# A Fourier and state-space mix on one core: the first loads from another queue, the vectors prepared later, a retuned order

## The chip, the cores and the metric

The kernel runs on one core of a Trainium2 chip. The metric is device time in microseconds (us) of one execution; the kernel before takes 328.49 us in the median of three runs (327.45, 328.49 and 333.03). The core's engines work at the same time, each through its own queue in order: TensorE (PE; its weight loads are listed as PEld), VectorE (DVE), ScalarE (ACT), GpSimd (POOL) and SyncE (SP). DMAs are issued from the queues of SP, ACT and POOL.

## The reference: what is computed

The input x has 2048 rows (tokens) and 1024 columns. Two results are computed from it and mixed by a gate, one number per token:

```python
g = sigmoid((x * gate_w).sum(-1, keepdims=True))
a = irfft2(rfft2(x) * (w_r + 1j * w_i))            # over both axes
Lam_bar = exp(exp(log_dt) * Lam)                   # 1024 complex states
h[t] = Lam_bar * h[t-1] + x[t] @ B_bar.T           # over 2048 steps
b = 2 * real(h @ C.T) + x * Dskip
out = g * a + (1 - g) * b
```

So `a` filters x in the frequency domain, and `b` is a diagonal state-space model with complex states. The five vectors that the change speaks of are Lambda_re, Lambda_im, log_dt, Dskip and gate_w, of 1024 elements each.

## The kernel before, in words

Both transforms are written as matrix products with constant cosine and sine matrices. x comes in as eight pairs of row blocks (`load_x`, line 206), sixteen blocks of 128 x 1024 in all. In the text the blocks are T0 to T15, and the steps of the first stage are called by the letters that the kernel uses:

- **T** (`turn_x`, lines 725 to 730): PE transposes a block in eight products into a PSUM tile `pt` (four buffers), ACT copies it into `xQ`. What the state-space part later multiplies is `xQ`, and it needs all sixteen blocks.
- **f** (`fold`, lines 732 to 745): DVE adds and subtracts halves of the block (`preT`, `sums`).
- **F** (`fd`, lines 353 to 367): eight products of the folded block with the constant `G` (the transform over columns) into a PSUM tile, which DVE or ACT copies into `X1` (line 364; DVE for blocks 0, 3, 5, 10 and 15).
- **S** (`s1`, lines 369 to 387): four products with the constant `T2`, a copy by DVE or ACT into `A1` (line 385), and a DMA to a scratch in DRAM.
- **h** (`unit`, lines 311 to 327): 32 products of `xQ` with B, a copy by ACT. After two of them DVE has a list of pieces for the recurrence (`recur`, lines 263 to 309: multiplications, scans), taken off the list by **v** (`vector`, line 332) as far as the next number of `SHARE` allows.
- **a** (`small`, line 901) and **t** (`make_tab`, line 219): small arithmetic on the five vectors, and the tables of the recurrence, on ACT, DVE and POOL.
- **g** (`gate`, line 778): 32 products for the gate, a copy by ACT.
- **b**, **c**, **2**, **w**, **k** issue loads; **s** is a step of the rest of the Fourier part; **|** marks the end of the table work.

F, S, g and the throwaway products write to one pool of two PSUM buffers (`psA`, tag "ps"), so a product has to wait until the copy of the tile before the last is done.

The order in which PE, DVE and ACT get their instructions is written out by hand in the string `ORDER` (lines 39 to 45), one letter per step; each engine executes its share of it strictly in turn. SP and POOL are ordered by a planner. After the string, the early tiles, the late tiles and the output follow in loops.

Ahead of the string stands the start (lines 756 to 772): eight throwaway products on zeros (`keep_warm(8)`), the loads, T0, f0, T1, f1, four more throwaway products, F0. Then come lines 848 to 867: the five vectors, which line 185 loads from ACT's queue as the first DMAs of all, are transposed by PE into a tile `vps` of the `pt` pool and turned into `vecT`, `vecF`, `gw32`, `dt`, `are`, `thp` and `r_sb` by DVE and ACT.

Of the kernel before, what the change touches and what calls it, by code (L numbers as in the profile page):

```python
# [32 lines left out]
    3.3, 6.2, 1.8, 5.9, 1.6, 0.9, 2.9, 1, 3.4, 4, 2.5, 5.4, 0, 4.8, 2.2, 4.1,  # L33
    2.1, 1.5, 6.8, 1.3, 3.8, 3.8, 2.7, 1.2, 6.2, 2.3, 4, 4.7, 1.8, 0.7, 2.8, 0.8,
    4.1, 4.9, 2.9, 6.4, 1.5, 3.8, 4, 1.6, 1.4, 2.5, 3.3, 1.8, 4.2, 2.7, 0.4, 0,
    4.4, 1.7, 4.8, 0, 2.4, 5.5, 3.5, 5.1, 4.2, 4.3, 4.7, 3.2, 4.3, 1.6, 6.7, 5,
    1.1, 4.1, 2.1, 7.1, 4.8, 4.3, 5.9,
)
ORDER = (
    "FTfSTbTTFTSbfbfbTTFfTSfTbbFbTbfbTwSTSTFTf2baFfabaSxatfbbbFhtStbt",  # L40
    "tfFfbStthttFShStttthfFfkttFtvttthtStvgSfFcFttShtvtcvtthtttcSFtth",
    "ttvFtcStttStt|cvvsccdchvhvvehvshhvshvhvshvhvshvsshvshvsshvshvssh",
    "vsvhshsvshvsshshvsvshvshvsshvsvhsshvshvshvhvhvsvshvsvshvsvshsvvs",
    "hvsvvshsvshvsivshvsvsvh",
# [74 lines left out]
def kernel(  # L119
# [64 lines left out]
    for i, src in enumerate((B_Lambda_re, B_Lambda_im, B_log_dt, B_Dskip, gate_w)):  # L184
        nc.scalar.dma_start(out=vec8[:, i, :], in_=src.rearrange("(j p) -> j p", p=P))
# [162 lines left out]
    def gfnet():  # L348
# [4 lines left out]
        def fd(j):  # L353
# [10 lines left out]
            (nc.vector.tensor_copy if j in (0, 3, 5, 10, 15) else nc.scalar.copy)(  # L364
# [391 lines left out]
    keep_warm(8)  # L756
    load_x(0, slice(0, 1))
    load_x(0, slice(1, 2))
    for part in (slice(0, 4 * K), slice(4 * K, 4 * K + 4 * H)):
        nc.sync.dma_start(out=fft["G"][:, part], in_=cG[:, part])  # L760
    load_T2(0, 2)
    load_x(1)
# [8 lines left out]
    keep_warm(4)  # L771
# [76 lines left out]
    vps = psX.tile([P, 5, 8], BF16, name="vps", tag="pt")  # L848
    for i in range(5):
        nc.tensor.transpose(out=vps[:, i, :], in_=vec8[:, i, :], identity=ident[0:8, 0:8])  # L850
    vecT = cpool.tile([P, 5, 8], BF16, name="vecT")
    nc.vector.tensor_copy(out=vecT, in_=vps)
    vecF = cpool.tile([P, 4, 8], FP32, name="vecF")
    nc.vector.tensor_copy(out=vecF, in_=vps[:, 0:4])
    lre, lim, dskT = vecF[:, 0], vecF[:, 1], vecF[:, 3]
    gw32 = tmp.tile([P, 8, 32], BF16, name="gw32")
    nc.vector.tensor_copy(out=gw32, in_=vecT[:, 4].unsqueeze(2).to_broadcast([P, 8, 32]))
    sp = cpool
    dt = sp.tile([P, 8], FP32, name="dt")
    nc.scalar.activation(out=dt, in_=vecF[:, 2], func=ACT.Exp)  # L860
# [3 lines left out]
    r_sb = sp.tile([P, 8], FP32, name="r_sb")  # L864
    nc.scalar.activation(out=r_sb, in_=are, func=ACT.Exp)
    tau_f = tmp.tile([P, TC], FP32, name="tau_f")
    nc.vector.tensor_copy(out=tau_f, in_=tau_i)

    def sincos(pool, ang, shape, sin_out, cos_out, nm):

# [154 lines left out]
```

## Time and profile before

| | |
|---|---|
| median of three runs | 328.49 us |
| profiled execution, whole time | 327.43 us |
| its span in the profile | 325.3 us |
| PE busy | 313.9 us (96%) |
| DVE busy | 286.0 us (88%) |
| ACT busy | 167.9 us (52%) |
| POOL busy | 39.7 us (12%) |
| data moved by DMA | 54.18 MB |

The span runs from the first instruction to the last landing; around it lie 327.43 - 325.3 = 2.13 us. "L318" in a row is line 318 of the kernel. A timeline row gives the start, the duration, the engine, the line, the operation, the tiles and how many instructions are merged; a bracket at its end says how long the engine had been idle and what ended that. The stages by time: the first blocks come in until about 18 us; the string up to `|` takes until about 82 us; from there PE goes through the recurrence's products and the rest of the Fourier part; the last product ends at 322.2 us.

### The profile page before, as it was taken

How to read it: one execution, taken by the hardware profiler on the slowest of the kernel's cores; microseconds unless marked ns; L12 is line 12 of the kernel's file. 1: busy time of each engine (PE TensorE's matmuls, PEld its weight loads, DVE VectorE, ACT ScalarE, POOL GpSimd, SP SyncE). 2: the span in 40 equal slices, each digit the busy share in tenths (PEclk: the TensorE clock that was granted, in tenths of full speed). 3: DMA queues.
4: the chain of work that ended last, by engine and by line, in shares of the span. 5: the costliest groups of instructions: out<-in, count | busy, mean ns of one | idle time of the engine just before them, and what ended most of it. 6: DMA issues, size and time to landing. Idle time of an engine off the chain costs nothing.

```text
span 325.3 us, 6698 instructions
## 1 busy us (share of the span) xinstructions
PE 313.9 (96%) x2739; PEld 207.8 (64%) x2739; DVE 286.0 (88%) x379; ACT 167.9 (52%) x215; POOL 39.7 (12%) x70
## 2 busy tenths in 40 slices
PE   8899899998999999999999999999999999999996
PEld 4555578475875665747474667779746866565554
DVE  2797998999999999999998799999999849999742
ACT  3699698845351146756675633556612244352510
POOL 1472112210000000000000000000000012235520
PEclk9999999999999999999999999999999999999999
DMA  6999999999979645698975537775122023769996
GB/s 225 415 161 210 260 182 241 165 177 127 310 169 182 109 122 123 194 249 230 228 207 132 163 102 258 158 215 177 34 73 90 0 21 51 126 95 144 169 176 192
DMA packets 79117, 54.18 MB, mean 167 GB/s; under 512 B 53832, under 2 KB 70736, under 8 KB 79088
## 3 DMA queue, kind: packets, MB, share of 16 engines
q1 hardware_dynamic: 74688, 50.04, 63.0%
q0 software_dynamic: 4320, 3.71, 11.7%
q8 instruction: 21, 0.34, 0.5%
q14 instruction: 8, 0.07, 0.1%
q10 hardware_dynamic: 80, 0.01, 0.0%
HBM read 24.90 MB, written 17.83 MB: 131 GB/s over the span
## 4 chain that ended last, share of the span: by engine, by line
PE 67%; DVE 23%; ACT 5%; DMA 2%; issue 2%; POOL 0%; POOLq 0%; ACTq 0%; DVEq 0%
PE psu L318 26%; PE ps_y L621 23%; DVE h L287 5%; PE ps_h L621 3%; PE ps_is L523 2%; PE ps_is L561 2%; DMA raw<-ye 2%; DVE h L275 2%; PE ps_y L625 1%; DVE X L364 1%; PE ps_s L499 1%; PE pt L728 1%; PE psw L754 1%; DVE su L272 1%; PE ps_q L636 1%
## 5 line engine op out<-in xcount | busy, mean ns | idle before, releaser
L318 PE MATMUL psu<-xQ,BT 128*128 128x256 bf16 x1024 | 116.2, 273 | 0.8 <-ACT ye L648 0.5
L318 PEld LDWEIGHTS <-BT 128*128 128x128 bf16 x1024 | 98.6, 98 | 17.3 <-issue 6.1
L621 PE MATMUL ps_y<-CT,h 128*128 128x512 bf16 x448 | 101.4, 379 | 0.0
L621 PEld LDWEIGHTS <-h 128*128 128x128 bf16 x496 | 47.3, 98 | 54.8 <-issue 3.3
L287 DVE TENSOR_TENSOR_SCAN h<-rz,h 128x2048 bf16<-128x2048 f32 (+1 forms) x20 | 70.9, 3562 | 0.3
L320 ACT CAST h<-psu 128x1024 bf16<-128x1024 f32 x32 | 32.3, 1010 | 52.8 <-PE psu L318 50.6
L275 DVE TENSOR_TENSOR h<-h,tab 128x4096 bf16<-128x4096 bf16 (+1 forms) x20 | 37.3, 1864 | 0.8
L676 POOL DMA_DIRECT2D BT<-y_scratch x10 | 12.0, 1199 | 202.0 <-DVE BT L670 191.5
L648 ACT ACTIVATE ye<-ps_y,omg 128x512 f32<-128x512 f32 x20 | 12.6, 684 | 39.1 <-PE ps_y L625 31.4
L272 DVE TENSOR_TENSOR xQ<-h,tab 128x4096 bf16<-128x4096 bf16 x12 | 27.4, 2288 | 2.5 <-ACT h L320 2.2
L504 ACT CAST X<-ps_s 128x1024 bf16<-128x1024 f32 x16 | 16.2, 1010 | 9.8 <-PE ps_s L499 8.9
L664 ACT ACTIVATE BT<-ps_id,gB 128x1024 bf16<-128x1024 f32 x14 | 15.3, 1112 | 9.4 <-PE ps_id L661 9.3
L358 PE MATMUL ps_fd<-G_sb,preT 128*128 128x512 bf16 x64 | 16.5, 379 | 2.5 <-DVE preT L739 1.3
L661 PE MATMUL ps_id<-raw,ZT 128*128 128x256 bf16 x128 | 16.1, 273 | 0.9 <-ACT BT L664 0.9
L729 ACT COPY xQ<-pt 128x1024 bf16<-128x1024 bf16 x16 | 15.5, 1052 | 2.5 <-PE pt L728 2.5
L563 ACT CAST ZT<-ps_is 128x1024 bf16<-128x1024 f32 x16 | 15.5, 1024 | 2.2 <-PE ps_is L561 2.2
L527 ACT CAST C<-ps_is 128x1024 bf16<-128x1024 f32 x16 | 15.4, 1018 | 0.0
L661 PEld LDWEIGHTS <-ZT 128*128 128x128 bf16 x128 | 12.1, 98 | 2.3 <-issue 1.1
L739 DVE TENSOR_TENSOR preT<-xQ 128x512 bf16<-128x512 bf16 x16 | 6.7, 420 | 7.7 <-ACT xQ L729 7.4
L375 PE MATMUL ps_s<-X,raw 64*128 64x512 bf16 x64 | 9.7, 380 | 2.9 <-DVE CT L385 1.6
L513 DVE TENSOR_TENSOR UV<-X,raw 128x2048 bf16<-128x2048 bf16 x8 | 9.4, 1218 | 3.5 <-PE ps_is L523 1.9
L697 ACT ACTIVATE ye<-ps_y,omg 128x512 f32<-128x512 f32 x8 | 5.2, 684 | 13.9 <-DMA raw<-ye 6.3
(199 smaller groups left out, 358.2 us busy)
## 6 DMA issues: line engine op xcount, KB each, us to landing
y_scratch<-ye SPq DMA_DIRECT2D x20, 256.0 KB, 2.5
Bb<-turn_scratch SPq DMA_DIRECT2D x16, 256.0 KB, 4.7
turn_scratch<-C SPq DMA_DIRECT2D x16, 256.0 KB, 2.9
raw<-turn_scratch SPq DMA_DIRECT2D x8, 512.0 KB, 4.3
CT<-in_A_x_dram SPq DMA_DIRECT2D x7, 512.0 KB, 6.6
out_dram<-BT SPq DMA_DIRECT2D x12, 256.0 KB, 5.3
BT<-y_scratch POOLq DMA_DIRECT2D x10, 256.0 KB, 5.9
turn_scratch<-CT SPq DMA_DIRECT2D x8, 256.0 KB, 3.9
```

What stands on the lines that cost most here:

```text
L272: nc.vector.tensor_mul(out=tmps["s"], in0=u[:, ::-1], in1=bc(i))
L275: nc.vector.tensor_mul(out=u, in0=u, in1=bc(i))
L287: nc.vector.tensor_tensor_scan(out=seg, data0=rz[:, js.start + j:js.start + j + m].rearrange("p j t -> p (j t)"), data1=seg, initial=0.0, ...
L318: nc.tensor.matmul(psu[:, j, :], lhsT=BT[4 * q + j][:, ri, d8, :], rhs=xQ[:, c, d8, :], start=(d8 == 0), stop=(d8 == 7))
L320: nc.scalar.copy(out=hs[c][:, ri, 4 * q:4 * q + 4].rearrange("p b (q j) -> p b q j", j=32), in_=psu.rearrange("p b (j q) -> p b q j", j=32))
L358: nc.tensor.matmul(ps[:, 1, :], lhsT=preTs[j][:, 4 + d4, :], rhs=Go[:, d4, :], start=(d4 == 0), stop=(d4 == 3))
L504: nc.scalar.copy(out=X2[b], in_=ps2[b])
L527: nc.scalar.copy(out=C1.rearrange("p h (c i) -> p h c i", c=2), in_=psc[t].rearrange("p h (i c) -> p h c i", c=2))
L563: nc.scalar.copy(out=ZT[:, 4 * kp:4 * kp + 4, :, 4 * G:4 * G + 4].rearrange("p (c r) n g -> p c r n g", c=2), in_=psz.rearrange("p c (g r ...
L621: nc.tensor.matmul(psy, lhsT=hs[c][:, ri, jb, P * tq:P * (tq + 1)], rhs=CT[ri][:, jb, 512 * dh:512 * (dh + 1)], start=(i == 0), stop=False)
L661: nc.tensor.matmul(pse[:, slot, :], lhsT=ZT_t[:, i, tb, :], rhs=fft["Gi"][:, i, :], start=(kb == 0), stop=(kb == 1))
L729: nc.scalar.copy(out=x_gjq[:, :, :, :, j, :].rearrange("p c d g q -> p d c g q"), in_=pt.rearrange("p d (c q g) -> p d c g q", c=NCH, g=2))
```

## The change

It touches the start, the place of the vectors' work, one copy, the order and the shares:

- `G` (768 KB) is issued from ACT's queue in three parts of 256 KB, ahead of the loads of x in the program, instead of from SP's in two parts (512 and 256 KB) behind the first pair of x.
- On SP's queue the second pair of x follows the first directly; then come the first rows of `T2`.
- The five vectors are loaded from POOL's queue, behind these loads in the program, and no longer from ACT's.
- 6 and 2 throwaway products instead of 8 and 4.
- The vectors' preparation becomes a function `vectors`, called by a new letter V in the string: behind T5 and ahead of T6 and F2.
- The copy of F15's result goes from DVE to ACT.
- The string is rearranged in places, with the same steps otherwise. In the first stage: T6 comes ahead of F2; T7 ahead of S1; f5 ahead of F3; f6 behind F4; T15 ahead of F5; the whole of `a` (a1 to a3, the long a3 with 22 small operations on DVE) stands ahead of S5, where a3 stood behind it; h5 ahead of g. Some loads c and some empty t move; one v moves by a step late in the string.
- 35 of the 71 numbers of `SHARE` differ (their sum goes from 232.8 to 236.6).

```diff
-    "FTfSTbTTFTSbfbfbTTFfTSfTbbFbTbfbTwSTSTFTf2baFfabaSxatfbbbFhtStbt",
-    "tfFfbStthttFShStttthfFfkttFtvttthtStvgSfFcFttShtvtcvtthtttcSFtth",
-    "ttvFtcStttStt|cvvsccdchvhvvehvshhvshvhvshvhvshvsshvshvsshvshvssh",
...
+    "FTfSTbTTVTFTSbfbfbTfFTSTbbFbTbffbTwSTSTTf2baFfaFaaSxtfbbbbFhttSt",
+    "tfFfbbSttfhttFShStttthfFkttttFtthtShtvvcgSfFFtSttvtcvtthtttSttFc",
+    "hcttvtFSttStt|vvtsccdchvhvcvehvshhvshvhvshvhvshvsshvshvsshvshvss",
...
     vec8 = tmp.tile([8, 5, P], BF16, name="vec8")
-    for i, src in enumerate((B_Lambda_re, B_Lambda_im, B_log_dt, B_Dskip, gate_w)):
-        nc.scalar.dma_start(out=vec8[:, i, :], in_=src.rearrange("(j p) -> j p", p=P))
...
-            (nc.vector.tensor_copy if j in (0, 3, 5, 10, 15) else nc.scalar.copy)(
+            (nc.vector.tensor_copy if j in (0, 3, 5, 10) else nc.scalar.copy)(
...
-    keep_warm(8)
+    keep_warm(6)
+    for part in (slice(0, 2 * K), slice(2 * K, 4 * K), slice(4 * K, 4 * K + 4 * H)):
+        nc.scalar.dma_start(out=fft["G"][:, part], in_=cG[:, part])
     load_x(0, slice(0, 1))
     load_x(0, slice(1, 2))
-    for part in (slice(0, 4 * K), slice(4 * K, 4 * K + 4 * H)):
-        nc.sync.dma_start(out=fft["G"][:, part], in_=cG[:, part])
+    load_x(1)
     load_T2(0, 2)
-    load_x(1)
+    for i, src in enumerate((B_Lambda_re, B_Lambda_im, B_log_dt, B_Dskip, gate_w)):
+        nc.gpsimd.dma_start(out=vec8[:, i, :], in_=src.rearrange("(j p) -> j p", p=P))
     load_x(2)
...
-    keep_warm(4)
+    keep_warm(2)
     fft["fd"](0)
...
+    def vectors():
+        vps = psX.tile([P, 5, 8], BF16, name="vps", tag="pt")
+        for i in range(5):
+            nc.tensor.transpose(out=vps[:, i, :], in_=vec8[:, i, :], identity=ident[0:8, 0:8])
+        nc.vector.tensor_copy(out=vecT, in_=vps)
+        nc.vector.tensor_copy(out=vecF, in_=vps[:, 0:4])
+        nc.vector.tensor_copy(out=gw32, in_=vecT[:, 4].unsqueeze(2).to_broadcast([P, 8, 32]))
+        nc.scalar.activation(out=dt, in_=vecF[:, 2], func=ACT.Exp)
+        nc.vector.tensor_mul(out=are, in0=dt, in1=lre)
+        nc.vector.scalar_tensor_tensor(out=thp, in0=dt, scalar=INV2PI, in1=lim, op0=ALU.mult, op1=ALU.mult)
+        nc.scalar.activation(out=r_sb, in_=are, func=ACT.Exp)
+        nc.vector.tensor_copy(out=tau_f, in_=tau_i)
...
+        "V": vectors, "2": lambda: load_T2(8, 16), "w": load_Wcols, "k": load_small, "|": front_done,
```

The first row of the string in words, from F1 to F3: before, PE gets F1 T2 S0 T3 T4 T5 F2 T6 S1 T7 T8 F3; after, F1 T2 S0 T3 T4 T5 V T6 F2 T7 S1 T8 F3.

## The prediction

> **What bounds the kernel now.** I read the page's first part (PE is busy for 96% of the span), then a table by stages, whose columns are the stretch, its length, the busy time of PE, PEld, DVE, ACT and POOL with instruction counts, the granted clock, the DMA share and GB/s:
>
> ```profile
> 0.00:1.22 1.22, 0.00 (x0) 0.00 (x1) 0.33 (x2) 0.00 (x0) 0.65 (x6) 1.00 0.00 0
> 1.22:82.00 80.78, 75.33 (x643) 49.77 (x644) 67.41 (x147) 59.21 (x81) 19.82 (x45) 1.00 1.09 219
> 82.00:322.20 240.20, 238.54 (x2098) 158.00 (x2096) 217.77 (x230) 108.69 (x135) 19.23 (x20) 1.00 0.65 151
> ```
>
> From 82 us on PE idles for 1.66 us in 240, and its steps there hardly change. So the change is worth what it moves the moment at which PE begins h8, the first product behind the string's `|` (81.85 us). Before that PE idles 1.22 us, then 80.78 - 75.33 = 5.45 us. The second view is PE's timeline of that stretch, with the waits named:
>
> ```profile
> 1.22 3.59 PE L754 MATMUL psw<-A 128*128 128x512 bf16 x8 [1.22 <-DVE A L749]
> 4.61 1.88 PE L728 MATMUL pt<-ident,CT 128*128 128x128 bf16 x16
> 6.32 1.04 PE L754 MATMUL psw<-A 128*128 128x512 bf16 x4
> 7.36 1.02 PE L358 MATMUL ps_fd<-G_sb,preT 128*128 128x512 bf16 x4
> ...
> 13.56 1.04 PE L358 MATMUL ps_fd<-G_sb,preT 128*128 128x512 bf16 x4 [0.69 <-DVE preT L739]
> ...
> 38.66 0.61 PE L375 MATMUL ps_s<-X,raw 64*128 64x512 bf16 x4 [1.29 <-DVE CT L385]
> ...
> 80.90 0.61 PE L375 MATMUL ps_s<-X,raw 64*128 64x512 bf16 x4 [1.11 <-DVE X L364]
> ```
>
> The waits name DVE and ACT: until 82 us the three engines bound each other. The ceiling of any gain is the 5.45 us and about 1.2 us of throwaway work, 6.6 us; 2% of 328.49 us, about what a measurement of this kernel can tell from no change, is 6.57 us.
>
> Third, ACT's timeline at the vectors, and the DMA list with the time to landing last:
>
> ```profile
> 10.59 0.21 ACT L860 ACTIVATE dt<-vecF 128x8 f32<-128x8 f32 x1 [2.95 <-DVE vecF L854]
> 11.03 0.21 ACT L865 ACTIVATE r_sb<-are 128x8 f32<-128x8 f32 x1 [0.23 <-DVE are L861]
> 11.14 0.99 ACT L364 CAST X<-ps_fd 128x1024 bf16<-128x1024 f32 x1
> 12.03 3.76 ACT L729 COPY xQ<-pt 128x1024 bf16<-128x1024 bf16 x4
> ```
>
> ```profile
> CT<-in_A_x_dram SPq DMA_DIRECT2D x2, 256.0 KB, 2.9
> G_sb<-c_G SPq DMA_DIRECT2D x1, 512.0 KB, 5.6
> Wp<-in_A_w_r_dram POOLq DMA_DIRECT2D x1, 7.5 KB, 5.9
> ```
>
> The vectors hold up ACT: F1's result is there at 10.44 (9.84 + 0.60), its copy starts at 11.14. G's first part, issued at 1.66, lands at 7.26; F0 begins at 7.36, though its fold was ready at 7.17. So G's landing is as late as the fold, and throwaways alone could not be cut with gain.
>
> **The change part by part.** I wrote the queues of PE, DVE and ACT one behind another, step for step, for both orders, each step at the later of "engine free" and "input ready plus 0.03". Occupancies are from the timeline: T 0.445 us on PE (at the early pace 0.86), F 1.30, S 0.54, h 3.50; a copy 0.90 on ACT and 1.13 on DVE; a fold 2 x 0.335 and 2 x 0.21 to 0.335; a3 2.65. For before this gives F0 at 7.29 (trace 7.36), F4 20.5 (21.13), h0 31.1 (31.77), h4 54.1 (54.88), F15 77.8 (77.78), h8 82.05 (81.85). So I use differences of two such lists only.
>
> *Start.* Eight throwaways begin every 0.427 us (T0 at 4.61 less 1.22, over 8); six end at 3.78. T0 then needs x's first 256 KB, which lands at 0.74 + 2.9 = 3.64 alone. Beside it now runs a part of G: 512 KB, as much as x's second part needed, which landed at about 4.15. I take T0 at 4.18 (-0.43); 3.78 (-0.85) if G takes nothing, 5.0 (+0.4) if two parts of G go ahead of x.
>
> In the stretch from 3.5 to 5.5 the DMA share was 0.60 to 0.80, while SP's queue stood idle from 2.95 to 3.62 waiting for earlier DMAs: there was room. [...]
>
> T0 on PE 0.86, its copy 1.02, its fold 0.42 bring F0 to 6.76 (-0.53); G's first two parts and x's first pair are 1 MB, which the GB/s of the windows up to 5.5 and the idle time filled move by about 6. The second group of throwaways, two warm ones of 0.21 less, lies beside T0's copy and fold: worth nothing by itself.
>
> *Vectors.* ACT's copies of F1 and T2 no longer stand behind `dt` and `r_sb`: f2 moves from 13.1 to 11.5. But V's tile takes the `pt` buffer of T2 and T6 that of T3, free at 12.4; T6 now stands ahead of F2, so F2 starts at 12.87 (-0.67) with T6 already done. V's own cost, 0.55 us of ACT (10.59 to 11.14) and about 0.7 us of DVE, is paid at 14 us instead. At F3 PE is 0.9 us ahead. On POOL five DMA issues come in front of the 8 table copies (L226); those also shift by 3 us, POOL idles before and nothing waits for POOL there. If that cover is gone, see the rivals.
>
> *Order.* Here the gain goes. f5 (1.46 us of DVE) now stands ahead of the copy of F3's result, and F4 waits for that PSUM buffer: from -0.9 to +0.46. a3, which waits for ACT's table load (1.28 us) and takes 2.65 us on DVE, now stands ahead of the copy of S5; F7 needs that buffer and waits 2.6 us instead of 0.75 in the trace's row at 30.47: h0 comes at +1.78. Then it is won back, since DVE has done a3: S7's wait of 1.29 falls by 0.6 (h1 +1.16); h5 ahead of g covers the gate's copy by ACT (S13 +0.17); F15's copy on ACT (0.90, ACT idle from 78.99) ends the wait of 1.11: S15 -0.5, of which the tile's next user gives back 0.37. **h8: -0.13 us.**
>
> With DVE and ACT 2% slower, or 0.06 us per handover, the same lists give -0.8 to -0.9, with both -1.4, because DVE has 1.13 us less to copy; with x late (T0 at 5.0) they give +0.7. I take -0.4, between the middle list and the slower ones. `SHARE` and the one moved v I cost at nothing: PE's order behind `|` is the same, and 1.66 us idle in 240 say that DVE keeps up; if not, each piece of the list that comes late costs PE up to a scan, 4.4 us. Profiled time 327.43 - 0.4 = **327.0 us**. The median of the runs shown lies 1.06 above its profiled execution, so up to 328.1 would be the same result.
>
> **The rivals.**
>
> *The front gain stays* (0.25). For: the two give-backs are waits for DVE, whose order of two short steps may be hidden where the trace's DVE is already late (f3 to f5 between 17.8 and 22). Without F4's and half of F7's loss, -0.4 - 1.36 - 0.7 = -2.5 us: 325.0 us.
>
> *The vectors come late, and it gets slower* (0.13). POOL's issues took 0.51 to 1.40 us each and landed 4.2 to 6.0 us later beside this traffic. From 1.6 us on, five of them end at 4.2 to 8.6 and land at 8.4 to 14.6. V's products stand in PE's queue ahead of T6, and PE is there at 11.8; every landing after 12.3 stops PE, DVE and ACT alike. At 14.6 the list gives +1.4 for h8, 2.3 worse than with an early landing: 327.43 + 1.4 = 328.8 us, and up to 330 if T0 is late too. Against it: the patterns of 0.1 KB took 0.52 us, which gives 8.6 to 9.
>
> *G beside x delays x* (0.08), so that the change doesn't do what it says: T0 at 5.0, h8 +0.7, 328.1 us.
>
> *PE stays at the slow pace* (0.06). The products ran at half pace until about 6.2: eight throwaways at 0.427 and 16 transposes in 1.71 us, then four throwaways in 0.86. [...]
>
> **How the numbers follow.** The forecast, give-back of the front's gain, 0.45, 327.0; the rivals as above; 0.03 for something not seen, such as SP's planner putting the loads of C behind others, which PE needs at 96 us. The range takes in the gain that stays (325.0, with 0.6 less for a T0 at 3.78) and late vectors: 324.4 to 330.5. No case but the unseen one passes 2% (below 321.9 or above 335.1): faster 0.02, same 0.95, slower 0.03.
>
> **What would show it.** T0 at about 4.2 and F0 at 6.8 on PE; ACT's copy of F1 at 9.6; F2 behind T6 near 13; a wait of over a microsecond at F4 and of over two at F7 (row L358, ended by DVE's copy L385); S15 without a wait for DVE; h8 between 80 and 83 us, and from there the same 240 us. It is wrong if PE waits at V, if a window behind 82 us has PE idle by more than 1 us more than now, or if h8 comes before 80.

## The result, and the profile after

The kernel after takes 331.54 us in the median of four runs (330.91 to 331.83); the kernel before takes 327.97 us, now with a fourth run (327.30). The ratio is 1.0113, with a 95% interval of 1.0082 to 1.0144: 3.6 us slower in the medians, short of the 2% bound but clear of the runs' scatter, and on the other side of the forecast of 327.0 us. The profiled execution after took 331.49 us with a span of 329.4, so 4.06 us more than the one before.

Where the time came from is read as the prediction reads it. First the table by stages of the kernel after (stretch, its length, busy time of PE, PEld, DVE, ACT and POOL, granted clock, DMA share, GB/s):

```profile
1.22:82.00 80.78, 74.22 (x608) 49.04 (x609) 63.67 (x145) 57.55 (x79) 21.80 (x50) 0.98 1.04 225
82.00:326.00 244.00, 241.27 (x2129) 159.47 (x2127) 220.97 (x232) 111.75 (x138) 19.25 (x20) 1.00 0.64 146
```

Up to 82 us PE now idles 80.78 - 74.22 = 6.56 us (5.45 before), and the clock granted there is no longer 1.00 but 0.98 in the mean. The last product now ends at 326.0 us; h8 begins at 85.47. From h8 to the last product it is 240.5 us, against 322.2 - 81.85 = 240.35 before. The account of the 4.06 us is therefore 3.62 at h8, 0.15 behind it and 0.3 between the last product and the end of the span.

PE's timeline of the stretch, in the kernel after (start, duration, line, tiles, count; the bracket is the idle time in front and what ended it). L726, L356, L359, L373 and L316 are the old L728, L358, L361, L375 and L318:

```profile
4.59 1.04 PE L726 MATMUL pt<-ident,CT 128*128 128x128 bf16 x8 [0.63 <-DMA CT<-in_A_x_dram]
5.95 1.03 PE L726 MATMUL pt<-ident,CT 128*128 128x128 bf16 x8 [0.32 <-DMA CT<-in_A_x_dram]
...
7.63 1.91 PE L356 MATMUL ps_fd<-G_sb,preT 128*128 128x512 bf16 x4
...
22.82 1.02 PE L356 MATMUL ps_fd<-G_sb,preT 128*128 128x512 bf16 x4 [0.92 <-ACT CT L383]
...
29.91 0.60 PE L359 MATMUL ps_fd<-G_sb,preT 128*128 128x256 bf16 x4
31.93 0.60 PE L373 MATMUL ps_s<-X,raw 64*128 64x512 bf16 x4 [1.42 <-DVE X L362]
33.46 1.79 PE L356 MATMUL ps_fd<-G_sb,preT 128*128 128x512 bf16 x4 [0.93 <-ACT X L362]
35.05 1.06 PE L359 MATMUL ps_fd<-G_sb,preT 128*128 128x256 bf16 x4
35.90 4.19 PE L316 MATMUL psu<-xQ,BT 128*128 128x256 bf16 x32
40.03 0.61 PE L373 MATMUL ps_s<-X,raw 64*128 64x512 bf16 x4
...
41.97 0.60 PE L373 MATMUL ps_s<-X,raw 64*128 64x512 bf16 x4
```

The same place in the kernel before, F6 to S6:

```profile
27.72 1.02 PE L358 MATMUL ps_fd<-G_sb,preT 128*128 128x512 bf16 x4
28.58 0.60 PE L361 MATMUL ps_fd<-G_sb,preT 128*128 128x256 bf16 x4
29.11 0.61 PE L375 MATMUL ps_s<-X,raw 64*128 64x512 bf16 x4
30.47 1.02 PE L358 MATMUL ps_fd<-G_sb,preT 128*128 128x512 bf16 x4 [0.75 <-ACT X L364]
...
31.77 3.66 PE L318 MATMUL psu<-xQ,BT 128*128 128x256 bf16 x32
35.35 0.61 PE L375 MATMUL ps_s<-X,raw 64*128 64x512 bf16 x4
```

Three things stand in the kernel after that the rows of before do not have. T0 and T1 now wait for x (the two rows ended by the DMA of CT), so T0 comes no earlier than before, and F0's first four products take 1.91 us instead of 1.02. Behind F6 (the 29.91 row, ending at 30.51) PE idles 1.42 us, does S5, idles 0.93 more and begins F7 at 33.46, 3.0 us later than before. And F7 and h0 (the row of 4.19) then run slowly: from 33.46 to S6 at 40.03 it is 6.57 us, against 35.35 - 30.47 = 4.88 before. S7 (41.97) in return has no wait at all. The sum to S6: +1.33 (start of F6, 29.05 against 27.72) + 1.66 (F6 to F7) + 1.69 (slow products) = +4.68; S7's wait of 1.29 and 0.08 more fall away: +3.31 at h1; +0.31 more up to h8. (The 22.82 row is F4; its wait of 0.92 is taken up behind the table of terms below.)

What ACT does in front of F7, in its timeline of the kernel after:

```profile
30.77 0.21 ACT L879 ACTIVATE a_kk<-ang 128x16 f32<-128x16 f32 x1
31.00 1.28 ACT L880 ACT_TABLE_LOAD   x1
32.30 0.22 ACT L880 ACTIVATE s2c<-ang 128x16 f32<-128x16 f32 x1
32.42 0.99 ACT L362 CAST X<-ps_fd 128x1024 bf16<-128x1024 f32 x1
```

The last row is the copy of F6's result; its PSUM buffer is the one that F7 needs. F6 ended at 30.51, so the copy could have started there; it starts at 32.42, because a1 with its table load of 1.28 us now stands ahead of F6 in the string and so ahead of its copy in ACT's queue. Before, this copy started first and the table load stood behind it:

```profile
29.29 1.12 ACT L364 CAST X<-ps_fd 128x1024 bf16<-128x1024 f32 x1
30.20 0.33 ACT L876 ACTIVATE a_kk<-ang 128x16 f32<-128x16 f32 x1
30.54 1.28 ACT L877 ACT_TABLE_LOAD   x1
```

The granted clock of the kernel after, in windows of 1 us, columns as in the first table:

```profile
33.00:34.00 1.00, 0.54 (x2) 0.25 (x2) 0.76 (x7) 0.62 (x2) 0.00 (x0) 0.79 1.10 128
34.00:35.00 1.00, 1.00 (x3) 0.30 (x2) 0.90 (x9) 0.00 (x0) 0.00 (x0) 0.50 0.76 146
35.00:36.00 1.00, 1.00 (x6) 0.70 (x5) 0.89 (x8) 0.00 (x0) 0.00 (x0) 0.50 1.28 300
36.00:37.00 1.00, 1.00 (x7) 0.69 (x6) 0.97 (x3) 0.85 (x1) 0.00 (x0) 0.51 1.00 295
```

The third number from the end is the clock: full up to 33.5, 0.50 for 3.4 us, and full again from 37. Half of these 3.4 us, 1.7, is what F7 and h0 take longer (1.69). That is the second price of the stall. In an execution of some 330 us it lowers the mean clock to about 0.995; this mean is the clock that is given with the runs below.

### The profile page after: what moved, and what is told of

Its sections match the earlier page's. It is cut to its first block, busy times and chain, and to the rows that moved or that the text cites. A ratio compares the mean times of both kernels' runs of the same rounds, so it can differ in the third digit from the quotient of the medians.

```text
span 329.4 us, 6695 instructions
## 1 busy us (share of the span) xinstructions
PE 315.5 (96%) x2735; PEld 208.5 (63%) x2735; DVE 285.3 (87%) x378; ACT 169.3 (51%) x216; POOL 41.7 (13%) x75
## 4 chain that ended last, share of the span: by engine, by line
PE 76%; DVE 9%; ACT 8%; DMA 3%; issue 2%; POOL 0%; SPq 0%; POOLq 0%; ACTq 0%
PE psu L316 32%; PE ps_y L619 22%; PE ps_fd L356 4%; PE ps_h L619 3%; DVE h L285 3%; PE ps_is L521 2%; PE ps_is L559 2%; DMA raw<-ye 2%; PE ps_fd L359 2%; ACT xQ L727 2%; DMA CT<-in_A_x_dram 1%; PE ps_y L623 1%; PE ps_s L497 1%; ACT X L362 1%; ACT h L318 1%
## 5 line engine op out<-in xcount | busy, mean ns | idle before, releaser
L316 PE MATMUL psu<-xQ,BT 128*128 128x256 bf16 x1024 | 116.9, 273 | 0.8 <-ACT ye L646 0.5
L316 PEld LDWEIGHTS <-BT 128*128 128x128 bf16 x1024 | 98.9, 98 | 18.0 <-issue 6.5
L318 ACT CAST h<-psu 128x1024 bf16<-128x1024 f32 x32 | 32.3, 1011 | 51.3 <-PE psu L316 49.1
L356 PE MATMUL ps_fd<-G_sb,preT 128*128 128x512 bf16 x64 | 18.1, 409 | 3.6 <-DVE preT L737 1.1
L362 ACT CAST X<-ps_fd 128x1024 bf16<-128x1024 f32 x12 | 12.1, 1006 | 7.9 <-PE ps_fd L359 7.9
L356 PEld LDWEIGHTS <-preT 128*128 128x128 bf16 x64 | 6.2, 102 | 10.7 <-issue 5.6
```

Source lines behind the costliest of these rows:

```text
L316: nc.tensor.matmul(psu[:, j, :], lhsT=BT[4 * q + j][:, ri, d8, :], rhs=xQ[:, c, d8, :], start=(d8 == 0), stop=(d8 == 7))
L318: nc.scalar.copy(out=hs[c][:, ri, 4 * q:4 * q + 4].rearrange("p b (q j) -> p b q j", j=32), in_=psu.rearrange("p b (j q) -> p b q j", j=32))
L356: nc.tensor.matmul(ps[:, 1, :], lhsT=preTs[j][:, 4 + d4, :], rhs=Go[:, d4, :], start=(d4 == 0), stop=(d4 == 3))
```

## The experiments

The theory after these views: the loss is (1) the table load ahead of F6's copy on ACT, (2) the clock's fall behind the resulting pause of PE, (3) a start that gains nothing because x is late and the slow pace lasts longer. The rivals: the prediction's own mechanism (a3 on DVE ahead of the copy of S5), the place of f5, the loads themselves, the throwaways. All ratios are to the kernel before, with 95% intervals. Rows of letters in the diffs are the part of `ORDER` that differs.

### Four undoings of one part each

The kernel after with 8 and 4 throwaway products again:

```diff
-    keep_warm(6)
+    keep_warm(8)
...
-    keep_warm(2)
+    keep_warm(4)
```

> The changed kernel with 8 and 4 throwaway products again, nothing else. Theory of the slow start: PE stands still before T0 and T1, and so runs at half pace until 9.3 us instead of 6.2; with eight throwaways, which end at 4.63 when x's first part lands at 4.54, the half pace ends by about 6.5, F0 takes 1.3 us instead of 2.3, T2 begins at about 10.3 instead of 11.24, and 0.5 to 1.0 us of the 3.6 us at h8 are won back. Theory of the order (the loss is made between F5 and h0): T2 may move, but h0 stays within 0.5 us of 35.9 and the time within 0.5 us of the changed kernel's 331.5.

Measured: 329.42 us, ratio 1.0068 (1.0049 to 1.0087). F0 ran at the full pace from 7.29 us, and T2 came at 9.89 (11.24 after, 10.27 before). S5 waited 1.92 us and F7 0.93, h0 came at 33.90. The runs were 329.18, 329.35 and 329.49 us at a clock of 1.0 and 330.51 at 0.995. At equal clock that is some 1 us better than the kernel after; the other half of the 2.1 us is that the clock fell less often (in one of four executions; in all four of the kernel after).

The kernel after with the loads as before (G on SP's queue in two parts behind the first pair of x, the vectors on ACT's):

```diff
+    for i, src in enumerate((B_Lambda_re, B_Lambda_im, B_log_dt, B_Dskip, gate_w)):
+        nc.scalar.dma_start(out=vec8[:, i, :], in_=src.rearrange("(j p) -> j p", p=P))
...
-    for part in (slice(0, 2 * K), slice(2 * K, 4 * K), slice(4 * K, 4 * K + 4 * H)):
-        nc.scalar.dma_start(out=fft["G"][:, part], in_=cG[:, part])
     load_x(0, slice(0, 1))
     load_x(0, slice(1, 2))
+    for part in (slice(0, 4 * K), slice(4 * K, 4 * K + 4 * H)):
+        nc.sync.dma_start(out=fft["G"][:, part], in_=cG[:, part])
+    load_T2(0, 2)
     load_x(1)
-    load_T2(0, 2)
-    for i, src in enumerate((B_Lambda_re, B_Lambda_im, B_log_dt, B_Dskip, gate_w)):
-        nc.gpsimd.dma_start(out=vec8[:, i, :], in_=src.rearrange("(j p) -> j p", p=P))
```

> The changed kernel with all loads issued as before: G from SyncE's queue in two parts behind x's first pair, the five vectors from ScalarE's queue first; throwaways 6 and 2, order and shares as changed. If G beside x is what makes T0 late: x's first part lands at about 3.6 again, T0 begins at 3.8 instead of 4.59, T1 without a wait, F0 at about 7.3 (then G's landing is last), T2 1 us earlier. If the order makes the loss: h0 moves by less than 0.5 us and the time stays within 0.7 us of 331.5; if the loads make it, the time comes down by 2 us or more.

Measured: 329.31 us, 1.0062 (1.0038 to 1.0087). T0 came at 3.75, but F0 only at 7.65, behind G (issued at 1.66, landed 5.8 us later): what x gains G loses. S5 waited 1.94 and F7 0.93 us; in the profiled execution (330.57 us, clock 0.995) the clock was 0.50 from 33.4 to 36.8 and h0 took 4.50 us; the three executions at 1.0 took 328.57 to 329.36. So 2.2 us of the 3.6 are back here too, which the expectation had put down to the loads. But PE ran F0 at full pace here (1.02 us) and T2 came at 10.25, 1.0 earlier than in the kernel after, and the clock fell in one execution of four instead of four; the loads alone cost nothing in the kernel before (below). That this run's gain lies in the pace and the clock, and not in the loads, is argued from these figures and not shown.

The kernel after with the segment from F5 to a3 in the order of before (F5 ahead of T15 and f8, F6 ahead of a1, S5 ahead of a3):

```diff
-TTf2baFfaFaaSxtf
+TFTf2baFfaaSxatf
```

> The changed kernel with one stretch of the order as before: T14 F5 T15 f8 (F5 ahead of T15 and f8), a0 and a1 behind F6, a3 behind S5. Theory of the order: f8 and a0 no longer stand ahead of the copy of F5 on DVE, nor the table load ahead of the copy of F6 on ACT; PE's waits at S5 (1.42) and F7 (0.93) fall below 1 us together, the granted clock stays at 1.00 between 33 and 37 us, h0 begins at 32.5 to 33.5 instead of 35.90, and the time falls by 2.5 to 3.5 us to about 328.5. Theory of the slow start: h0 falls by at most 1 us and the time stays at 330.5 or above.

Measured: 328.76 us, 1.0034 (1.0018 to 1.0049): 2.8 us of the 3.6 are back. F7 waited 0.75 us as before, the clock was 0.999 or 1.0 in all six runs, h0 came at 31.29; S7's wait was 1.76. The runs lie at 327.73 and 327.85 and at 328.68 to 329.19; the profiled one (327.85) had the full pace already at T0 and T2 at 9.43. With the same loads and throwaways the kernel after had T2 at 11.24, and the next run has it at 11.75. So the start of the changed kernel is worth from -0.8 to +1.5 us against the 10.27 of before, as the pace turns. The 10.27 is one profile too: in three others whose start is that of the kernel before, T2 comes at 9.85, 10.23 and 11.18.

The kernel after with six throwaway products on PE behind F6:

```diff
-TTf2baFfaFaaSxtf
+TTf2baFfaFWaaSxtf
...
+    def mid_warm():
+        psw = psX.tile([P, K], FP32, name="psm", tag="pt")
+        for i in range(6):
+            nc.tensor.matmul(psw, lhsT=ident, rhs=fft["G"][:, 0:K], start=True, stop=True)
```

> The changed kernel with six throwaway products behind F6 (1.3 us, in a wait of PE of 1.6 us, into a free tile of the transposes' pool). If the fall of the granted clock to 0.50 between 33.4 and 36.9 comes from PE's idle time there: the clock stays at 1.00, F7 takes 1.3 instead of 2.4 us, h0 3.5 instead of 4.13, S6 begins at about 38.3 instead of 40.03, and h8 comes 1 to 1.8 us earlier. If the clock falls for another reason, or DVE and ACT set the pace there anyway, S6 may move but h8 stays within 0.5 us.

Measured: 330.36 us, 1.0085 (1.0068 to 1.0102). The clock stayed at 1.00 from 33 to 37 us and at 0.998 or 0.999 over every run; F7 began even later than in the kernel after, at 34.07, but ran in 1.02 us, h0 took 3.66 and h8 came at 84.74, 0.7 earlier; counted from F6, which came 0.5 later in this profile, it is 1.2 earlier. Useless work made the kernel 1.2 us faster in the medians (329.87 to 330.67 against 330.91 to 331.83). The fall is a price of its own.

### Which letter in the segment

Only F5 ahead of T15 and f8 (so that its copy on DVE stands ahead of f8):

```diff
-TTf2baFfaFaaSxtf
+TFTf2bafaFaaSxtf
```

> The changed kernel with only F5 put ahead of T15 and f8 again (T14 F5 T15 f8), a1 and a3 left where the change has them. Theory: of PE's stall between F6 and h0 one half is the copy of F5 behind f8 and a0 on DVE (f8 has to wait until F5 has read its buffer, the copy then begins 1.5 us after F5's end), the other the copy of F6 behind the table load on ACT. Then S5 comes right behind F6, F7 still waits 1.3 to 2.5 us for ACT, h0 begins at 33 to 35, and the time lies between the changed kernel (ratio 1.011 to before) and the run with the whole stretch restored (1.0034): about 1.006 to 1.009. Rival, that only one of the two is the cause: ratio at or below 1.004 (F5 is all of it) or at or above 1.010 (F5 is none of it).

Measured: 330.88 us, 1.0095 (1.0065 to 1.0125). S5 no longer waits, but F7 starts where it did, its wait now 2.84 us in one piece. The copies of F5 (DVE) and F6 (ACT) hold up PE side by side, and to mend the first alone brings little. In this profile the clock stayed at 1.00 behind the 2.84 us; in the three other executions it was 0.988 to 0.995.

Only a0 and a1 behind the copies of F5 and F6, and a3 behind S5:

```diff
-TTf2baFfaFaaSxtf
+TTf2bFaFfaaSxatf
```

> The other half alone: the changed kernel with a0 and a1 behind the copies of F5 and F6 and a3 behind S5, as before, F5 left behind T15 and f8. Theory of two halves: the copy of F6 comes straight after F6, F7's wait for ACT falls below 0.5 us; S5 still waits for the copy of F5, which f8 (0.8 us) holds up; h0 between 32.5 and 34, ratio 1.004 to 1.008. Rival, only one cause: at or below 1.004 (the table load is all of it) or at or above 1.010 (none of it).

Measured: 329.93 us, 1.0042 (1.0016 to 1.0069). F7 did not wait, h0 came at 33.38 (35.90 after), the clock was 0.998 to 1.0 in all seven runs; the start of the profiled one had the half pace until 9.6.

Only a1 behind F6, a2 and a3 left ahead of S5. This tells the table load from a3, which the prediction had named:

```diff
-TTf2baFfaFaaSxtf
+TTf2baFfFaaaSxtf
```

> The kernel after with one letter moved: a1 (with ACT's table load) behind F6 instead of ahead of it; a2 and a3 stay ahead of S5, f9 ahead of F6. If the table load in front of F6's copy on ACT is the cause: the copy begins at about 30.6, F7 follows S5 without a wait at 32.5, h0 at 33.8 (35.90 now), clock 1.00 at 33 to 37 us; 329.7 us, some 1.8 less than the kernel after. If a3 on DVE ahead of the copy of S5 is the cause, as the prediction had it: F7 still waits over 2 us, h0 at 35.5 or later, 331.3 us. Part of the gain can be lost again at S7 (DVE's copies behind a3).

Measured: 330.04 us, 1.0065 (1.0048 to 1.0082), 1.5 us better than the kernel after. PE's timeline of this kernel:

```profile
31.88 0.61 PE L373 MATMUL ps_s<-X,raw 64*128 64x512 bf16 x4 [1.29 <-ACT X L362]
32.42 1.04 PE L356 MATMUL ps_fd<-G_sb,preT 128*128 128x512 bf16 x4
...
33.73 3.66 PE L316 MATMUL psu<-xQ,BT 128*128 128x256 bf16 x32
...
41.02 0.61 PE L373 MATMUL ps_s<-X,raw 64*128 64x512 bf16 x4 [1.69 <-DVE CT L383]
```

F7 follows S5 without a wait although a3 still stands ahead of the copy of S5, and h0 is 2.2 us earlier. So a1's table load was F7's wait, not a3. (S5's wait stays; the trace names ACT's copy, which ends at 31.83, but S5's buffer is F5's, whose copy on DVE ends at 31.76.) The gain of 2.2 at h0 is 1.3 at h8, 84.17: S7 waits 1.69 us again for DVE's copy behind a3.

The same the other way round: the kernel before with a1 ahead of F6, and a3 ahead of S5 (f9 passes F6 as well, but f runs on DVE alone and F6 on PE and ACT, so no queue changes by that):

```diff
-TFTf2baFfabaSxatf
+TFTf2bafaFbaaSxtf
```

> The kernel before with only the small arithmetic moved as in the change: a1 ahead of F6 and a3 ahead of S5, so that the table load (1.28 us) stands on ScalarE ahead of the copy of F6. Theory: F7 waits 2 to 3 us for that copy instead of 0.75, h0 begins at 33.5 to 34.5 instead of 31.77, h8 1 to 2 us later, and in part of the runs the granted clock of the whole run falls to 0.995 (3.5 us at half); ratio 1.003 to 1.009. Rival, that this stretch costs only together with the late start: ratio below 1.002.

Measured: 330.84 us, 1.0091 (1.0059 to 1.0123). These moves of `a` in the kernel before make a loss nearly as large as the whole change (1.0113). ACT's timeline of it, and PE's row at F7:

```profile
30.73 1.28 ACT L877 ACT_TABLE_LOAD   x1
...
32.15 0.99 ACT L364 CAST X<-ps_fd 128x1024 bf16<-128x1024 f32 x1
```

```profile
33.19 1.02 PE L358 MATMUL ps_fd<-G_sb,preT 128*128 128x512 bf16 x4 [2.85 <-ACT X L364]
```

F7 waits 2.85 us instead of 0.75. The profiled execution took 330.01 us at a clock of 1.0; the three others, at 0.995, took 330.32, 331.36 and 331.61.

The same with six throwaways behind F6, which divides wait and fall:

```diff
-TFTf2baFfabaSxatf
+TFTf2bafaFWbaaSxtf
```

> The kernel before with a1 ahead of F6 (as in the one-move kernel above, 330.84 us) and six throwaway products on PE behind F6, into a tile of the pt pool. The wait of F7 for ACT's copy of F6 stays about 2.8 us long, of which PE is now busy for 1.3. If the fall of the granted clock to 0.5 behind this wait is a second price, paid in most executions: clock 1.00 from 33 to 37 us and 0.998 or more over every run, h0 3.5 us long, 329.9 us, with no run above 330.4. If the wait is the whole price and the clock changes nothing: 330.8 us as without them. If the throwaways themselves delay F7: 331 us or more.

Measured: 329.18 us, 1.0042 (1.0027 to 1.0057), all four runs at 0.998 to 1.0. PE's timeline:

```profile
29.02 1.46 PE L953 MATMUL psm<-G_sb,ident 128*128 128x512 bf16 x6
30.41 0.61 PE L375 MATMUL ps_s<-X,raw 64*128 64x512 bf16 x4
32.63 1.02 PE L358 MATMUL ps_fd<-G_sb,preT 128*128 128x512 bf16 x4 [1.61 <-ACT X L364]
33.93 3.66 PE L318 MATMUL psu<-xQ,BT 128*128 128x256 bf16 x32
```

F7 still waits for the same copy, and PE idles 1.61 us of that time instead of 2.85. The wait alone costs 1.5 us over the kernel before; with the clock free to fall it was 3.1 (330.84 against 327.79). F6 began 0.6 us earlier in this profile than in the one without the throwaways, which they can't have caused (there G landed 6.5 us after its issue and F0 came at 8.27, here at 7.31); how much of the 1.66 us between the two is the clock is therefore taken from the runs below.

### The start and the loads by themselves

The kernel before with 6 and 2 throwaways, nothing else:

```diff
-    keep_warm(8)
+    keep_warm(6)
...
-    keep_warm(4)
+    keep_warm(2)
```

> The kernel before with 6 and 2 throwaway products, nothing else. G lands at 7.26 there whatever PE does, so F0 cannot start before 7.3: if the throwaways only fill time, T0 begins at 3.8 (x is there at 3.64) and the ratio is 0.998 to 1.002. If fewer of them let the half pace last into F0 and F1 (as in the changed kernel, until 9.3), T2 begins 0.5 to 1.2 us later than 10.27 and the ratio is 1.002 to 1.004, with a spread over the runs of about 1 us.

Measured: 327.71 us, 1.001 (0.9991 to 1.0029). T0 came at 3.76, F0 waited 0.53 us for G until 6.81. Six runs at a clock of 0.998 to 1.0 took 326.77 to 327.77; four at 0.994 or 0.995 took 328.65 to 329.29.

The kernel before with G on ACT's queue in three parts and the vectors on POOL's, prepared where they were:

```diff
-    for i, src in enumerate((B_Lambda_re, B_Lambda_im, B_log_dt, B_Dskip, gate_w)):
-        nc.scalar.dma_start(out=vec8[:, i, :], in_=src.rearrange("(j p) -> j p", p=P))
...
+    for part in (slice(0, 2 * K), slice(2 * K, 4 * K), slice(4 * K, 4 * K + 4 * H)):
+        nc.scalar.dma_start(out=fft["G"][:, part], in_=cG[:, part])
     load_x(0, slice(0, 1))
     load_x(0, slice(1, 2))
-    for part in (slice(0, 4 * K), slice(4 * K, 4 * K + 4 * H)):
-        nc.sync.dma_start(out=fft["G"][:, part], in_=cG[:, part])
+    load_x(1)
     load_T2(0, 2)
-    load_x(1)
+    for i, src in enumerate((B_Lambda_re, B_Lambda_im, B_log_dt, B_Dskip, gate_w)):
+        nc.gpsimd.dma_start(out=vec8[:, i, :], in_=src.rearrange("(j p) -> j p", p=P))
```

> The kernel before with only the loads changed: G in three parts from ScalarE's queue beside x, the vectors from GpSimd's (they land at 7 to 8.8), prepared at their old place behind F0, throwaways 8 and 4. If x beside G costs: x's first parts land at 4.5 and 5.9, T0 at 4.6 as before, T1 0.4 us later, F0 no later than 7.4 because G is there; the vectors' products, ready at 8.8, wait up to 0.2 us. Ratio 0.999 to 1.003. If G beside x were what costs the 3.6 us, the ratio would be 1.006 or above.

Measured: 327.67 us, 0.9997 (0.9987 to 1.0007): no difference. T0 4.73, F0 7.59, T2 10.50, h8 81.61. The DMA list of the kernel after (KB of one, median us to landing), against 2.9 us for x's two parts and 5.6 for G's 512 KB before:

```profile
CT<-in_A_x_dram SPq DMA_DIRECT2D x2, 256.0 KB, 4.3
G_sb<-c_G ACTq DMA_DIRECT2D x3, 256.0 KB, 4.6
```

G comes earlier and x later, by about as much: in the profile after, G's first two parts (512 KB) have landed by 5.7 us, against 7.26 for its first 512 KB before; x's two parts land at 4.54 and 5.9, against 3.64 and 4.15. Beside G on the other queue x's parts took 4.3 us instead of 2.9.

### What is left when these parts are undone

The kernel after with 8 and 4 throwaways and the segment as before:

```diff
-TTf2baFfaFaaSxtf
+TFTf2baFfaaSxatf
...
-    keep_warm(6)
+    keep_warm(8)
...
-    keep_warm(2)
+    keep_warm(4)
```

> Eight and four throwaway products and the stretch of the order restored, all else as changed: G beside x, vectors from GpSimd and at V, f5 ahead of F3, h5 ahead of g, F15's copy on ScalarE, the shares. If half pace at the start and that stretch are the whole loss, the ratio is 0.998 to 1.003, h8 at 81.0 to 82.0, and runs no longer spread over more than 0.8 us. If the loads or the rest of the order cost something by themselves, it stays at 1.004 or above.

Measured: 328.43 us, 1.0022 (1.0006 to 1.0039); nine of ten runs 328.0 to 328.75 at 0.998 or more, one 330.68 at 0.994. F7 waits 0.75, h0 comes at 31.61, S7 waits 1.78, h8 82.13.

That and the loads as before:

```diff
-    for part in (slice(0, 2 * K), slice(2 * K, 4 * K), slice(4 * K, 4 * K + 4 * H)):
-        nc.scalar.dma_start(out=fft["G"][:, part], in_=cG[:, part])
...
+    for part in (slice(0, 4 * K), slice(4 * K, 4 * K + 4 * H)):
+        nc.sync.dma_start(out=fft["G"][:, part], in_=cG[:, part])
+    load_T2(0, 2)
     load_x(1)
-    load_T2(0, 2)
...
```

> The run before with the loads as before as well. If the loads cost by themselves (x's first pair lands at 4.5 and 5.9 instead of 3.6 and 4.2), T1 and F0 come 0.3 us earlier and the time falls by 0.3 to 1 us against the run before; if DVE's list sets the moment of S7 whatever the start does (38.65 with T2 at 9.43, 38.66 with T2 at 10.27), the two agree within 0.4 us.

Measured: 331.01 us, 1.0092 (1.0075 to 1.0109), far from both expectations. G's first part took 6.6 us to land behind x, and F0 came at 8.41, T2 at 11.01; with the same loads it landed after 5.0 to 6.5 us in other profiles. Then PE's row at S7:

```profile
40.87 0.61 PE L375 MATMUL ps_s<-X,raw 64*128 64x512 bf16 x4 [2.41 <-DVE CT L385]
```

Behind this wait the clock was at 0.50 from 41.5 to 45 us, and all four runs were at 0.993 or 0.994: a fall in another place, behind another engine's copy. Why the old loads make S7 wait 2.41 us here instead of 1.78, in a kernel where the loads should be free, stays open.

The kernel with 8 and 4 throwaways and the segment, and the string's first row as before too (V stays behind T5):

```diff
-FTfSTbTTVTFTSbfbfbTfFTSTbbFbTbffbTw
+FTfSTbTTVFTSbfbfbTTFfTSfTbbFbTbfbTw
```

> The kernel after with 8 and 4 throwaways, the segment of F5 to a3 as before (328.43 us with these two) and, new, the first row of the string as before: T6 behind F2, T7 behind S1, f5 behind F3, f6 as before; V stays behind T5. Work left out: none. If the rest of 0.2% against the kernel before comes from the order between V and F4: h8 at 81.9 or earlier, 327.8 us. If it comes from V in its new place, the h5 and g exchange, or the shares: 328.4 us, h8 at 82.1 with F4 earlier and the gain lost by S7. If T6 ahead of F2 was a gain: 329 us.

Measured: 329.06 us, 1.0028 (1.0013 to 1.0043), in two groups: four runs of 327.60 to 327.80 at a clock of 0.998 to 1.0, and seven of 328.97 to 329.74 at 0.993 to 0.995. The profiled execution of this run took 543 us at a clock of 0.559 and is left aside. The same kernel again, to see what separates the groups:

> The same kernel as the one with the first row as before, whose profile was taken in an execution at a clock of 0.559. Its other executions lie at 327.60 to 327.80 us (clock 0.998 to 1.0) and at 328.97 to 329.74 (clock 0.993 to 0.995). If the fall of the clock is again what separates them, and again comes behind a wait of PE: a profile at 327.7 us shows clock 1.00 throughout 2 to 86 us and h8 before 82.0; one at 329.2 us shows about 3.5 us at 0.50 behind the longest wait, of S7 for DVE's copy of S5 near 40 us, and h8 near 83.5. If the two groups differ in something else, the profile at 329.2 us shows the clock at 1.00 up to h8, or a late start of F0.

Measured: 328.17 us, 1.0013 (0.9989 to 1.0037); four runs of 327.25 to 327.64 at 0.998 or 1.0, four of 328.69 to 329.64 at 0.992 to 0.995. The profiled one is of the second group (328.81). Its timeline of PE and its windows, from 38 to 42 us:

```profile
30.34 3.66 PE L316 MATMUL psu<-xQ,BT 128*128 128x256 bf16 x32
...
38.31 1.04 PE L373 MATMUL ps_s<-X,raw 64*128 64x512 bf16 x4 [2.37 <-DVE CT L383]
39.28 4.72 PE L316 MATMUL psu<-xQ,BT 128*128 128x256 bf16 x32
```

```profile
38.00:39.00 1.00, 0.69 (x4) 0.13 (x3) 0.58 (x2) 1.00 (x4) 0.92 (x2) 0.53 0.78 176
39.00:40.00 1.00, 1.00 (x6) 0.54 (x5) 1.00 (x4) 1.00 (x4) 0.00 (x0) 0.50 0.75 150
40.00:41.00 1.00, 1.00 (x7) 0.69 (x6) 0.97 (x4) 1.00 (x2) 0.00 (x0) 0.50 1.16 263
41.00:42.00 1.00, 1.00 (x9) 0.82 (x8) 0.96 (x2) 0.64 (x1) 0.00 (x0) 0.77 0.99 269
```

h0 comes at 30.34, 1.4 us earlier than in the kernel before. DVE's copy of S6 does not follow, so S7 waits 2.37 us instead of 1.29 and takes back 1.1 of it; and at the end of this wait the clock falls, S7 and h1 take 0.43 and 1.06 us longer, and more is lost than was won. That sum, 1.49, is about the distance of the groups.

Last, S6 moved forward in the string among the t behind h0, to bring this copy forward: past two t in that kernel, past one in the kernel before:

```diff
-FhttSt
+FhSttt
```

```diff
-FhtStbt
+FhSttbt
```

> The kernel with 8 and 4 throwaways, segment and first row as before, and S6 ahead of the two table pieces behind h0 instead of behind them, so that DVE's copy of S6 stands behind a3 alone. Theory: that kernel's earlier start (h0 at 30.34 instead of 31.77) was lost at S7, which waited 2.37 us for this copy, and this wait made the clock fall in about half of the executions. Then the copy starts at about 34.7 instead of 37.0, S7 waits 0.5 us at most, h1 comes at 37.2 to 37.8 (39.28), the clock stays at 1.00 in all but one or two executions, and the time is 326.2 to 326.8 us, 0.3 to 0.4% under the kernel before. Rival: the tables come 1.2 us late and PE, ACT or DVE wait for them before h8; h8 at 81.6 or later and 327.6 us.

> The kernel before with S6 ahead of the two table pieces. Theory: S7's wait of 1.29 us for DVE's copy goes, h1 at 38.0 to 38.3 (39.20), 326.3 to 326.8 us. Rival (the list between h0 and h8 has its own pace, set by DVE's tables, so that PE waits for it later): the gain is lost by S13 or S15, 327.6 us.

Measured: 328.88 us, 1.0027 (1.0002 to 1.0051), and 327.76 us, 1.0003 (0.9976 to 1.0030). The edit missed its aim. DVE's copy starts at 37.00 in the first kernel, where it had started at 37.04:

```profile
35.72 0.69 DVE L877 TENSOR_TENSOR ang<-ang,rot_kk 128x512 f32<-128x512 f32 x1
36.33 0.42 DVE L737 TENSOR_TENSOR preT<-xQ 128x512 bf16<-128x512 bf16 x1
36.66 0.42 DVE L738 TENSOR_TENSOR sums<-xQ 128x512 bf16<-128x512 bf16 x1
37.00 1.22 DVE L383 CAST CT<-ps_s 128x1024 bf16<-128x1024 f32 x1
```

The table piece and the fold in front of it belong to letters that stand ahead of h0, not to the two that were moved. So neither expectation was put to the test, and whether S7's wait could be turned into time stays open. The first of the two has the same timing as the kernel that it changes: three runs of 327.65 to 327.68 at 0.999 or 1.0, nine of 328.72 to 329.81 at 0.993 to 0.995. Over the three runs with this timing, 11 executions without a fall average 327.60 us and 20 with one 329.14: **1.54 us for one fall of the clock.**

A side experiment on the S7 and S15 waits in the kernel before: the copies of S6 and F15 go from DVE to ACT:

```diff
-            (nc.vector.tensor_copy if j in (0, 3, 5, 10, 15) else nc.scalar.copy)(
+            (nc.vector.tensor_copy if j in (0, 3, 5, 10) else nc.scalar.copy)(
...
-            (nc.vector.tensor_copy if j in (0, 1, 3, 5, 6, 9) else nc.scalar.copy)(out=A1, in_=psa)
+            (nc.vector.tensor_copy if j in (0, 1, 3, 5, 9) else nc.scalar.copy)(out=A1, in_=psa)
```

> The kernel before with the copies of F15 and of S6 on ScalarE instead of VectorE. S7 waits 1.29 us for VectorE's copy of S6, which stands behind the tables' arithmetic, while ScalarE is idle from 36.47; S15 waits 1.11 us for VectorE's copy of F15. If these two waits are what PE loses there, S7 comes 0.8 to 1.1 us earlier and h8 1.0 to 1.6 us, ratio 0.995 to 0.998. If the tables set the pace, S7 is earlier but S9 to F12 wait instead, and the ratio stays at 0.998 to 1.001.

Measured: 328.17 us, 1.0013 (0.9999 to 1.0027): no gain. S7 then waits 1.56 us for ACT, whose copy stands behind table work as DVE's did.

## Why the prediction was wrong

**Right: the frame.** The change is worth what it moves h8 by; behind it hardly anything changed (240.5 us against 240.35), so the new shares and the moved v cost nothing there. With throwaways, segment and first row undone, the changed kernel at full clock takes 327.60 us, as the kernel before does (327.6 to 327.7 in these comparisons): loads, V in its new place, F15's copy, the rest of the order and `SHARE` together are worth about zero at full clock. Also right: the vectors, issued from POOL at 1.53 to 4.26 us, landed by 8.8, and nothing waited at V; with throwaways and first row undone, F2 comes at 12.55, 1.0 earlier than before (forecast 0.67).

The terms of the sum, as changes against before (for h8 the list gave -0.13, and -0.4 was taken):

| | forecast | measured in the profile |
|---|---|---|
| T0 | -0.43 | -0.02 |
| F0 | -0.53 | +0.27, at half pace |
| F2 | -0.67 | +1.22 |
| F4 | +0.46 | +1.69 |
| h0 | +1.78 | +4.13 |
| h1 | +1.16 | +3.31 |
| h8 | -0.13 (-0.4) | +3.62 |

**Right in kind: F4's wait.** f5 ahead of the copy of F3's result was forecast to lose 1.36 us between F3 and F4. DVE begins that copy at 21.75, 1.4 us after F3's end, F4 waits 0.92, and F4 slips 1.09 further than F3 did (+0.60 to +1.69). What is wrong in the +0.46 comes from ahead of F3.

**Wrong: "T0 at 4.18".** x's first part landed at 4.54 beside G and T0 came at 4.59, midway between the forecast and the rival's 5.0; little came of it: the loads alone measure 0.9997. From T0 to F0 the sum names 0.86, 1.02 and 0.42, which give 6.48; the other 0.28 of its 6.76 has no item.

**Wrong: the pace.** "PE stays at the slow pace" was a rival with 0.06. No run ahead of the result had fewer throwaways, so the 0.06 was the author's estimate. It came true in the profiled execution: F0's first four products took 1.91 us (1.02 before), T2 came 1.0 us late, and with 8 and 4 throwaways T2 1.35 us earlier than that. Which of the two groups of throwaways matters was not tried. It is not lost every time: with the changed start, T2 came at 9.43 in one profile and at 10.79 to 11.75 in five.

**Wrong: "a3 ... now stands ahead of the copy of S5; F7 needs that buffer and waits 2.6 us".** The idle time was nearly of the forecast size (1.42 + 0.93 = 2.35 us behind F6), but the engine and the letter were not. In a pool of two buffers F7 takes the one of F6, not of S5, as the row of before at 30.47, ended by ACT's copy (X L364), already said; F6's copy runs on ACT, and a1's table load stood ahead of it. Moving a1 alone took F7's wait away while a3 stayed. The step counted the table load as something that a3 on DVE waits for, and not as an instruction in ACT's queue with a copy behind it. S5's wait for DVE's copy of F5, behind f8, which itself waits for F5, was not in the sum either.

**Missing: the clock's fall.** No step and no rival had it. The sum treats a pause of PE as its length; here 2.35 us of pauses cost 1.69 us more in the products behind them. The pace at the start had a rival, the pause that the prediction itself forecast at F7 had none. This is the largest single term that was left out: 1.2 us by the throwaways behind F6, 1.5 by the two groups of runs.

**Wrong: "Then it is won back".** From h1 to h8 the list regains 1.29 us (1.16 to -0.13), the trace loses 0.31. Of S7's wait the whole 1.29 went, where 0.6 was forecast. But h5 ahead of g won nothing: PE waits 0.65 us in one piece around the gate instead of 0.21 and 0.39. And F15's copy on ACT leaves S15 a wait of 0.62 instead of 1.11, with 0.31 given back two rows later:

```profile
84.16 0.61 PE L373 MATMUL ps_s<-X,raw 64*128 64x512 bf16 x4 [0.62 <-ACT X L362]
85.07 0.16 PE L427 MATMUL Wrev_ps<-Wc,JP_sb 128*128 128x4 bf16 x1 [0.31 <-ACT A_last L383]
```

**The account.** Of the 3.6 us in the medians, the segment from F5 to a3 carries 2.8 when undone alone; 1.2 of it is the clock, by the run with throwaways behind F6. The throwaways carry 2.1 when undone alone, 1 of it at equal clock, and the loads, undone alone in this kernel, 2.2. These parts overlap, since an earlier start also changes whether the clock falls: segment and throwaways together give 3.1. The first row of the string carries the rest, about 0.8 at full clock (328.0 to 328.75 against 327.25 to 327.80); in the medians its undoing gains nothing sure (329.06, 328.17 and 328.88 against 328.43), because the clock then falls in 20 of 31 executions. What stays open is where the clock falls in the four of ten runs of the kernel before with 6 and 2 throwaways, since the profile of that kernel shows no fall; and no version here was clearly faster than the kernel before.

## What to carry to other kernels

Where engines execute in a fixed order, a moved step is costed on every engine that it issues to, with its table load: here 0.22 us of work (the row of `s2c`) brought 1.28 us of table load in front of a copy for which the bounding engine waits. In this kernel a pause of PE of 2.20 to 2.85 us had to be costed at its length plus, in 30 of 43 executions, 1.5 to 1.7 us for the half pace behind it; runs that split into two groups by granted clock were the sign of it. An earlier start is worth only what the next wait lets through, and when it lengthens that wait it can make the kernel slower: the undoing of the first row took S7's wait from 1.78 to 2.20 and 2.37 us in its profiles, and the clock fell in 20 of 31 executions.

## What the runs showed of the hardware

In the five profiles that show the granted clock at 0.50 the longest single pause of PE was 1.42, 1.94, 2.20, 2.37 and 2.41 us; in two others with pauses of 2.84 and 2.85 us the clock stayed at 1.00. Longest single pause of PE between 26 and 44 us in the profiled execution of each kernel, and how many of its executions had a mean clock of 0.996 or less (the kernel before with 6 and 2 throwaways, 1.34 us and 4 of 10, doesn't fit and is left open above):

| kernel | longest pause, us | executions with the fall |
|---|---|---|
| after, six throwaways behind F6 | 0.93 | 0 of 4 |
| before | 1.29 | 3 of 98, at 331.75 to 334.42 us |
| before, S6 past one t | 1.31 | 0 of 11 |
| before, G on ACT's queue, vectors on POOL's | 1.39 | 0 of 10 |
| before, S6 and F15 copied by ACT | 1.56 | 0 of 10 |
| before, a1 and a3 early, six throwaways behind F6 | 1.61 | 0 of 4 |
| after, a1 behind F6 | 1.69 | 0 of 4 |
| after, segment as before | 1.76 | 0 of 6 |
| after, segment and 8 and 4 | 1.78 | 1 of 10 |
| after, a0, a1 and a3 later | 1.91 | 0 of 7 |
| after, 8 and 4 (a second pause of 0.93 follows) | 1.92 | 1 of 4 |
| after, loads as before (the same) | 1.94 | 1 of 4 |
| segment, 8 and 4, first row (three runs) | 2.20 and 2.37 | 20 of 31 |
| segment, 8 and 4, loads as before | 2.41 | 4 of 4 |
| after, F5 early | 2.84 | 3 of 4 |
| before, a1 and a3 early | 2.85 | 3 of 4 |
| after (1.42 and 0.93 with 0.6 us of work between) | 1.42 | 4 of 4 |

The fall lasts 3.4 us in each of the five profiles (in the kernel after from 33.58 to 36.98). In the 3.4 us before it PE was busy for 1.00 to 1.29 us in all five; and the fall begins between 0.25 us before the end of the pause and 0.67 us after it, so it is not the pause's end that starts it.

The pace at the start varied too, and the granted clock did not show it: in the profiles before and after it reads 1.00 from the first product at 1.22 until 33 us, while eight transposes took 1.03 or 1.04 us at the slow pace and 0.61 or 0.62 at the full one. The earliest turn to the full pace is in the profile of the kernel with segment, 8 and 4 and the loads as before, where the 16 transposes from 4.31 us already took 1.06; the latest in the kernel after with six throwaways behind F6, where F0's last four products, from 9.65 us, still took 0.96 instead of 0.60.
